# A state-space layer and a gated convolution on one core: weights loaded in smaller pieces, zeros multiplied ahead of the data, and a new order of work

## The chip, the cores and the metric

The kernel runs on 1 core of one Trainium2 chip. The time is the device time of one execution in microseconds. "Span" is the length of the profiled execution in the trace; it is about 1.8 to 1.9 us shorter than the time of the same execution.

## The reference, cut to what matters

Two layers on sequences of 2048 steps and 640 channels, put side by side:

```python
# A: a diagonal complex state space, 640 states
Lam_bar = exp(dt * Lam);  Bu = x @ (B_bar.T)          # complex
for t in range(L): h = Lam_bar * h + Bu[:, t];  hs.append(h)
y_a = 2.0 * real(hs @ C.T) + x * Dskip
# B: a four-tap shift convolution of k, times v, then a 2048-long causal convolution
kv  = sum_t shift(k, t) * shift_k[:, t] * v
y_b = q * (causal_conv(kv, ssm_k) + kv * ssm_D)
return concatenate([y_a, y_b], -1)
```

Three things are enough. Side A needs x transposed, multiplied by B ("B products"), and the results of neighbouring steps joined by small products with rotation matrices M (powers of Lam_bar). Those matrices are built on the chip, in *sets*. Side B needs the shift convolution on VectorE and then many 64-wide products ("s1", "s2", "i1", "i2") on TensorE with two tables R and W.

## The kernel before

The kernel gives every operation a name and a function. A text, ORDER, then lists all of them; each engine works through its own operations in that order. A letter behind a slash chooses the engine (A ACT, D VectorE, G GpSimd, S SyncE for DMAs), and a number behind @ a buffer.

```python
def place(self, text):
    for word in text.split():
        word, _, slots = word.partition("@")
        name, _, e = word.partition("/")
        o = ops[name]
        o.eng = letter[e] if e else next(iter(o.alts))
        assert o.deps <= done, name
        ...
```

The operations that the argument touches:

```python
# ci1: one large integer product on GpSimd, for the cosine tables
self.op("ci1", {"POOL": 2.4}, lambda e: self.nc.gpsimd.tensor_tensor(out=civ(0), in0=civ(0), in1=..., op=ALU.mult), r=["ph"], ...)

# a set: five rotation matrices, two inputs from SBUF, on VectorE or GpSimd
def f(e, h):
    self.eng[e].tensor_tensor(out=mt[:, js, :]..., in0=E[:]..., in1=sap()[:, js, :]..., op=ALU.mult)
for h in range(parts):
    op(f"set_{key}_{h}", alts, lambda e, h=h: f(e, h), r=["E", dep], w=[f"M_{key}_{h}"])

# a unit of side A: ten B products twice (dn0, dn1), an eviction (e1), three rotations (m1), an eviction (e3)
op(f"dn{b}_{u}", {"PE": mm_cost(512, 5)}, f, r=[f"B{h}", f"x{hf}{b}", "Qz", "Bfree"], w=[f"pu{b}_{u}"], bufs=[pt], ...)
self.evac(f"e1_{u}", 768, ...)
op(f"m1_{u}", {"PE": 0.335}, f1, r=[f"h_{u}", f"M_1_{h}", f"M_2_{h}", f"M_3_{h}"], w=[f"pu1_{u}"], ...)
self.evac(f"e3_{u}", 256, ...)

# B through the transposing DMA, in two halves
for h in range(2):
    for u, ap in enumerate((self.A_B_re, self.A_B_im)):
        ...  # nc.sync.dma_start_transpose(out=self.BT[:, :, u, 320 * h:320 * h + 320], in_=ap[320 * h:320 * h + 320, :]...)

# side B's table for group G: its load (hst) and a tap added to it (dtap), which the s1 products wait for
op(f"hst{G}", {"SP": 0.4, "POOL": 1.2}, lambda e: self.eng[e].dma_start(...), w=[f"sth{G}"], ...)
op(f"dtap{G}", {"POOL": 0.26, "DVE": 0.1}, lambda e: self.eng[e].tensor_tensor(..., op=ALU.add), r=["Dm"], w=[f"sth{G}"], ...)
```

"wm0" is a scaling of half of a 64-wide table for W, "den" six tiny operations that lead to the last set, "sk", "cv", "cs" and "ca" the shift convolution.

## Time and profile before

| | before |
|---|---|
| time, median of 3 runs | 202.42 us (200.48 to 203.7) |
| span of the profiled run | 200.5 us |
| TensorE busy | 185.7 us (93%) |
| first B product starts | 11.93 us |
| first rotation (L231) starts | 19.93 us |
| gaps of TensorE behind that | 4.05 us |
| last matmul ends | 196.80 us |

The prediction below shows the page, TensorE's waits and the chain, and reads them. In the timeline (start and duration in us, engine, line, operation, tiles, shapes, count) these rows of VectorE and GpSimd come from the time just ahead of the first rotation and behind it:

```profile
14.70 0.75 DVE L492 TENSOR_TENSOR R<-vs,mk 128x256 bf16<-128x256 f32 x2
16.54 2.63 DVE L422 TENSOR_TENSOR M<-E,ss 128x640 bf16<-128x640 bf16 x2
19.09 0.95 DVE L239 CAST hb<-ps 128x768 bf16<-128x768 f32 x1
...
18.50 4.21 POOL L422 TENSOR_TENSOR M<-E,ss 128x640 bf16<-128x640 bf16 x3
...
33.12 0.17 DVE L387 TENSOR_TENSOR den<-lpar 128x10 f32<-128x10 f32 x1
```

R's two halves take 0.75 us together, done before GpSimd starts with its sets. "den" waits until 33 us, behind the whole convolution of the first group, and takes 0.17 us for its first operation. In the same trace the two operations of wm0 stand from 7.63 us on and take 0.81 and 0.69 us.

### The profile page before, as it was taken

How to read it: one execution, taken by the hardware profiler on the slowest of the kernel's cores; microseconds unless marked ns; L12 is line 12 of the kernel's file. 1: busy time of each engine (PE TensorE's matmuls, PEld its weight loads, DVE VectorE, ACT ScalarE, POOL GpSimd, SP SyncE). 2: the span in 40 equal slices, each digit the busy share in tenths (PEclk: the TensorE clock that was granted, in tenths of full speed). 3: DMA queues.
4: the chain of work that ended last, by engine and by line, in shares of the span. 5: the costliest groups of instructions: out<-in, count | busy, mean ns of one | idle time of the engine just before them, and what ended most of it. 6: DMA issues, size and time to landing. Idle time of an engine off the chain costs nothing.

```text
span 200.5 us, 8859 instructions
## 1 busy us (share of the span) xinstructions
PE 185.7 (93%) x4043; PEld 136.3 (68%) x4043; DVE 168.1 (84%) x264; ACT 148.1 (74%) x175; POOL 20.6 (10%) x35
## 2 busy tenths in 40 slices
PE   0599999979999999699999999999999999999982
PEld 0465566747777678467657777676787878788771
DVE  7899899876899999949988899788959999877540
ACT  4979998978899888389986749896967679752011
POOL 8056500700000000000000000100000010001010
PEclk9999999999999999999999999999999999999999
DMA  5999997999999999969995068509334334998985
GB/s 167 239 152 132 231 180 167 245 159 210 219 180 171 167 217 206 247 153 215 210 196 133 5 152 252 134 22 189 89 147 103 96 80 105 170 234 160 229 226 140
DMA packets 109959, 33.74 MB, mean 168 GB/s; under 512 B 107106, under 2 KB 108642, under 8 KB 109922
## 3 DMA queue, kind: packets, MB, share of 16 engines
q1 hardware_dynamic: 109668, 32.52, 83.9%
q8 instruction: 31, 0.51, 1.1%
q0 software_dynamic: 224, 0.66, 0.9%
q14 instruction: 6, 0.05, 0.1%
q10 hardware_dynamic: 30, 0.00, 0.0%
HBM read 9.19 MB, written 7.86 MB: 85 GB/s over the span
## 4 chain that ended last, share of the span: by engine, by line
PE 72%; DMA 14%; DVE 6%; ACT 3%; SPq 2%; issue 1%; POOL 0%; DVEq 0%; POOLq 0%; ACTq 0%
PE ps L806 20%; PE ps L658 17%; PE ps L909 9%; PE ps L945 8%; PE ps L231 4%; DMA s<-s 4%; PE ps L1001 4%; DMA s<-in_B_v_dram 4%; PE ps L233 4%; PE ps L1037 3%; DMA s<-in_A_x_dram 3%; DMA s<-in_B_ssm_k_dram 3%; DVE s L239 2%; PE ps L810 2%; ACT s L237 2%
## 5 line engine op out<-in xcount | busy, mean ns | idle before, releaser
L237 ACT CAST s<-ps 128x1024 bf16<-128x1024 f32 x86 | 84.1, 1018 | 16.9 <-PE ps L945 6.4
L658 PE MATMUL ps<-xT,BC 128*64 128x512 bf16 x400 | 49.1, 383 | 0.1
L806 PE MATMUL ps<-BC,hb 128*128 128x320 bf16 x240 | 36.4, 300 | 0.0
L658 PEld LDWEIGHTS <-BC 128*64 128x64 bf16 x400 | 22.3, 110 | 15.1 <-issue 0.9
L806 PEld LDWEIGHTS <-hb 128*128 128x128 bf16 x240 | 21.9, 98 | 8.7 <-issue 0.3
L968 DVE TENSOR_TENSOR s<-s,s 128x2048 bf16<-128x2048 bf16 x20 | 24.4, 1222 | 2.0 <-ACT s L237 0.7
L909 PE MATMUL ps<-R,s 64*64 64x128 bf16 x1280 | 22.5, 218 | 2.9 <-POOL s L831 1.8
L237 ACT CAST yo<-ps 128x640 bf16<-128x640 f32 x12 | 8.4, 698 | 22.7 <-PE ps L810 18.5
L909 PEld LDWEIGHTS <-s 64*64 64x64 bf16 x1280 | 18.7, 107 | 8.1 <-issue 3.7
L239 DVE CAST s<-ps 128x1024 bf16<-128x1024 f32 x14 | 17.0, 1220 | 8.3 <-PE ps L909 2.7
L945 PE MATMUL ps<-s,Wre 128*64 128x128 bf16 x320 | 21.4, 221 | 0.0
L763 DVE TENSOR_TENSOR hb<-ps,hb 128x512 bf16<-128x512 f32 x30 | 19.1, 684 | 2.8 <-PE ps L231 1.6
L945 PE MATMUL ps<-s,Wim 128*64 128x128 bf16 x320 | 21.2, 219 | 0.0
L945 PEld LDWEIGHTS <-Wre 128*64 128x64 bf16 x320 | 18.2, 110 | 2.5 <-issue 0.5
L884 DVE TENSOR_TENSOR s<-s,s 128x2048 bf16<-128x2048 bf16 x15 | 18.3, 1222 | 1.0 <-ACT s L876 0.7
L945 PEld LDWEIGHTS <-Wim 128*64 128x64 bf16 x320 | 18.1, 110 | 1.1
L1044 DVE TENSOR_TENSOR s<-ps,s 128x1024 bf16<-128x1024 f32 x10 | 11.8, 1216 | 4.1 <-PE ps L1037 3.9
L237 ACT CAST hb<-ps 128x768 bf16<-128x768 f32 x17 | 13.7, 808 | 1.1 <-PE ps L658 1.1
L968 DVE TENSOR_TENSOR s<-s 128x1024 bf16<-128x1024 bf16 x20 | 13.8, 688 | 0.3
L231 PE MATMUL ps<-hb,M 128*64 128x256 bf16 (+1 forms) x136 | 13.3, 296 | 0.0
L1037 PE MATMUL ps<-Ct,s 128*64 128x64 bf16 x640 | 11.6, 196 | 0.8 <-DMA s<-s 0.7
L1037 PEld LDWEIGHTS <-s 128*64 128x64 bf16 x640 | 11.1, 113 | 1.9 <-DMA s<-s 0.9
(157 smaller groups left out, 261.4 us busy)
## 6 DMA issues: line engine op xcount, KB each, us to landing
s<-in_B_ssm_k_dram SPq DMA_DIRECT2D x5, 512.0 KB, 4.7
kvd<-s SPq DMA_DIRECT2D x5, 512.0 KB, 4.4
s<-kvd SPq DMA_DIRECT2D x5, 512.0 KB, 5.6
s<-in_B_q_dram SPq DMA_DIRECT2D x5, 512.0 KB, 4.4
out_dram<-s SPq DMA_DIRECT2D x5, 512.0 KB, 5.1
out_dram<-yo SPq DMA_DIRECT2D x12, 160.0 KB, 2.8
s<-in_A_x_dram SPq DMA_DIRECT2D x2, 640.0 KB, 4.8
out_dram<-yo POOLq DMA_DIRECT2D x4, 160.0 KB, 3.4
```

The source lines that it names most:

```text
L231: self.nc.tensor.matmul(out[h], lhsT=lhsT[:, h], rhs=rhs, **k)
L237: self.nc.scalar.copy(out=out, in_=in_)
L239: self.eng[e].tensor_copy(out=out, in_=in_)
L658: nc.tensor.matmul(P[64 * ri:64 * ri + 64, b, :], lhsT=self.BT[:, k, ri, 64 * j:64 * j + 64], rhs=self.xT[:, k, hf, 2 * b:2 * b + 2, :].re ...
L763: v.tensor_tensor(out=hv(r), in0=self.P(p2)[:, 0, :].rearrange("p (h m) -> p h m", h=2), in1=hv(r), op=ALU.add)
L806: nc.tensor.matmul(P[:, part, 0:320], lhsT=hap(j), rhs=self.CT[:, j, c0:c0 + 320], start=(j == 0), stop=False)
L884: op(f"ca{j}{G}{h}", {"DVE": dve_tt(W_)}, lambda e, c=c, tt=tt: v.tensor_tensor(out=c(), in0=c(), in1=tt(), op=ALU.add), r=[f"tm{G}{h}"], ...
L909: nc.tensor.matmul(P[64 * ri:64 * ri + 64, r, 128 * b4:128 * b4 + 128], lhsT=d[64 * r:64 * r + 64, 4 * qd + b4, a0, :], rhs=self.R[64 * r: ...
L945: nc.tensor.matmul(P[64 * pi:64 * pi + 64, ri, 128 * k4:128 * k4 + 128], lhsT=W[:, kp, pi, :], rhs=A[:, kp + 16 * pi, :], start=True, stop ...
L968: v.tensor_tensor(out=o, in0=a, in1=b, op=op_)
L1037: nc.tensor.matmul(P[64 * ah:64 * ah + 64, b // 8, 64 * (b % 8):64 * (b % 8) + 64], lhsT=Z[:, 16 * h + b, 64 * ri:64 * ri + 64], rhs=self. ...
L1044: v.tensor_tensor(out=o, in0=self.P(pt)[:].rearrange("p s (b a c) -> p a (s b) c", b=8, a=16), in1=o, op=ALU.mult)
```

## The change

Its intent: start TensorE's clock with products of zeros while x is still on its way; load the first half of B in two pieces so that x's second half comes earlier; and use an order for all engines that was found with VectorE and GpSimd excluding each other at SBUF.

```diff
@@ setup @@
+        warm = self.g.buf("P", "warm", 1)
+        def f_warm(e):
+            for _ in range(8):
+                nc.tensor.matmul(self.P(warm)[:, 0, :], lhsT=self.xT[:, 0, 1, 0, 0:128], rhs=self.xT[:, 0, 1, 0:2, :]..., start=True, stop=True)
+        op("wz", {"POOL": 0.45, "DVE": 0.3}, lambda e: self.eng[e].memset(self.xT[:, 0, 1, 0:2, :], 0.0), w=["x10", "x11", "wz"])
+        op("warm", {"PE": 1.9}, f_warm, r=["wz", "x10", "x11"], w=["warm"], bufs=[warm], due=-35)
@@ a_B @@
-        for h in range(2):
+        for h, (lo, n) in enumerate(((0, 128), (128, 192), (320, 320))):
...
@@ a_unit @@
-  r=[f"B{h}", ...
+  r=[f"B{0 if j < 2 else 1 if j < 5 else 2}", ...
@@ ORDER: all of it is new; the words from the phases to the first taps @@
-x121 fi mk rn ph ci1 ld_sk/S dn0_2_0@4 x130 ex10/D trig dn0_0_0@6 B11 ex14/D ws1@4 R dn1_2_0 rc ss dn1_1_0@0 set_3_0/D
-set_2_0/G dn1_0_0 e1_2_0/A dn1_4_0@2 set_1_0/D ws0@5 k0@6 kz0/G set_1_1/G x131 dn0_4_0 e1_0_0/D hst0/S@2 m1_2_0 x120 set_3_1/G
-dn0_1_0 e3_2_0/D e1_4_0/D m1_0_0 dn1_8_0@4 ct@3 set_2_1/G e3_0_0/D e1_1_0/D dn0_8_0 sk x101 cv300/D@4 dn1_9_0@6 set_4_1/D
-m1_1_0 dn0_9_0 cs200/D@3 v0@5 e1_8_0/A dtap0/D set_8_1/D m1_4_0 e3_1_0/A m1_8_0 e3_4_0/A ca200 s1h03@0,4 ...
+B00 ex10/D ph dn0_2_0@4 ex14/D Dm1/S Ct ld_sk/S trig B20 dn0_4_0@6 ex12/D ws1@3 rc dn1_4_0 ss wm0 dn1_2_0 B21 dn1_1_0@2
+e1_4_0/D e1_2_0/A dn0_1_0 x120 set_2_0/D R dn0_0_0@0 x100 den x110 e1_1_0/D x101 hst0/S@4 ws0@5 kz2/G@6 ci1 set_3_0/G
+set_8_0/G set_1_0/G set_12_0/G m1_4_0 m1_2_0 set_2_1/G dn1_0_0 e3_2_0/D e3_4_0/A m1_1_0 sk e1_0_0/A dn0_9_0@4 cs200/D@2 ct@3
+cv300/D@3 dn1_3_0@6 x130 ca200 dn1_9_0 e3_1_0/D cs100/D dn0_3_0 set_3_1/D dn1_8_0@2 e1_9_0/A ca100 x131 e1_3_0/A m1_0_0
+e3_0_0/D x121 x111 v0@1 kz1/G@5 set_4_1/G set_1_1/G set_8_1/G set_12_1/G set_4_0/G m1_9_0 dn0_8_0 e3_9_0/D dtap0/G cs000/D
...
```

## The prediction

> **What bounds the kernel now.** I read the page first (its busy shares), then TensorE's waits, then the chain that ended last, then the timeline of the head, where the change is aimed.
>
> ```profile
> PE 185.7 (93%) x4043; PEld 136.3 (68%) x4043; DVE 168.1 (84%) x264; ACT 148.1 (74%) x175; POOL 20.6 (10%) x35
> PE ps L607 <- DMA s<-in_A_x_dram: 7.0, 2, 5.0
> PE ps L909 <- POOL s L831: 1.8, 1, 1.8
> PE ps L909 <- ACT s L237: 1.1, 1, 1.1
> PE ps L1037 <- DMA s<-s: 0.7, 1, 0.7
> ```
>
> The kernel is TensorE-bound: 185.7 of 200.5 us busy. The waits account for nearly all the rest: 5.0 us until the first half of x lands, 2.0 for its second half, 1.8 at 82 us, 1.1 at 43 us, 0.7 near the end, and 3.7 us from the last matmul (196.8 us) to the span's end. So a new order can win only (a) the head, (b) the gaps at 43, 82 and 191 us, (c) time in which TensorE is busy but slow.
>
> The head, from the chain of waits and the timeline:
>
> ```profile
> 4.19 5.45 DMA s<-in_A_x_dram
> 9.68 2.31 PE ps L607 x20
> 11.99 8.10 PE ps L658 x35
> 20.09 0.33 PE ps L231 x3
> ```
>
> ```profile
> 1.54 1.23 POOL L577 IOTA s<- 128x1280 int32 x1
> 1.63 1.33 DVE L461 TENSOR_SCALAR phs<-ws,rowa 128x32 int32<-128x32 int32 x2
> ...
> 11.50 2.33 POOL L578 TENSOR_TENSOR s<-s,ph 128x1280 int32<-128x1280 int32 x1
> 11.55 2.31 DVE L487 TENSOR_SCALAR mk<-mk 128x4 f32<-128x4 f32 x1
> ...
> 16.59 1.90 POOL L422 TENSOR_TENSOR M<-E,ss 128x640 bf16<-128x640 bf16 x1 [2.76 <-DVE ss L412]
> ```
>
> Two things to see. TensorE never stops between 9.68 us and 42.5 us, but it starts slow: 20 transposes take 2.31 us. Counted by window, L658:
>
> ```profile
> 11.92:13.00 1.08, 1.07 (x6) 0.49 (x8) 1.00 1.17 156
> 13.02:14.10 1.08, 1.08 (x12) 0.55 (x10) 1.00 1.28 257
> ```
>
> (matmuls in parentheses): 6 in the first 1.08 us, 12 in the next, while the granted-clock column says 1.00 in both. So there is a cold start which that column does not show. And VectorE is held[...]: a tensor_scalar of four elements a partition takes 2.31 us beside a 2.33 us GpSimd product and ends with it, where its neighbours take 0.15 us.
>
> **What the Trainium skill says.** "TensorE: Matmul & The Clock Gate", Part 1: the array runs at half clock until a free-running window of about 3.4 us has been busy, and the matmuls issued until then run cold. The trace agrees: transposes start every 0.107 us up to 11.7 us, and from 13 us on, pairs of 512-column matmuls start every 0.216 us instead of the first ones' 0.427. Part 4 of that page says transposes do not count as activity; this trace rather speaks against it, since only 0.9 us of ordinary matmuls precede the speed-up at about 12.8 us. "SBUF — State Buffer", "SBUF: two separate sides": GpSimd and VectorE share a port pair under an exclusive lock, held for a whole instruction, against VectorE's two-port modes and, for GpSimd operations that read SBUF, two-input ones. The rows above agree; so does a set product on GpSimd, 1.90 us beside VectorE's own and 1.25 us alone (at 20.2 us). The same section warns that descriptors of DMAs issued from GpSimd are held by that lock; the few such transfers of before (3.4 us to landing against 2.8 from SyncE for the same output tiles) show it at most weakly.
>
> **The change, part by part.**
>
> *Zeros ahead of the data.* One memset (about 0.2 us, VectorE, at about 1.1 us) and eight 512-column matmuls. Cold, they start every 0.427 us: 8 x 0.427 = 3.4 us, from about 1.3 to 4.8 us, inside the 5.0 us wait, so free. They do not delay x. With the transposes that follow from 5.0 us the array should be at full speed at some point between 5 and 8 us, depending on where the window lies. What was cold in before: 40 transposes x (0.107 - 0.054) = 2.1 us and two pairs x 0.21 = 0.4 us. The first 20 are followed by a wait for x anyway, so on the path are 20 x 0.053 + 0.4 = 1.5 us.
>
> *B's first half in two pieces.* In before 320 rows (0.41 MB) of B go between x's two halves on the DMA queue; now 192 rows (0.25 MB). Transposes moved about 0.28 MB/us, so 0.6 us less stands in front, and SyncE's issue of that piece falls from 1.97 us to about 1.2 (192/320). x's second half should land at about 8.2 us instead of 9.68, with a wide margin. The remaining 128 rows are first needed after four products of 1.08 us. So the first B product can start at about 8.2 + 1.1 (20 warm transposes) + 0.2 = 9.5 us instead of 11.9: 2.4 us earlier.
>
> *The order.* I read it engine by engine. TensorE's operations are the same but for the zeros. I count changes between tilings (64-column, 64-row, full) along its sequence: 82 in before, 72 now. In the chain each change costs about 0.11 us (ten matmuls of L658 take 1.20 us after L909 against 1.08 after their own kind; L806 1.47 against 1.36): 10 x 0.11 = 1.1 us saved. The transfer of the third h tile (512 KB), which left SyncE at 78.1 us and caused the 1.8 us gap at 82, now stands ahead of two C pieces and of the first Z transpose in SyncE's list: that gap should close. Between ACT and VectorE 26 evacuations and scalings go one way and 14 the other; eleven set and tap operations go from VectorE to GpSimd, two back. My sum is about +2 us on VectorE and -6 on ACT: neither becomes the bound. Ten DMA issues move from SyncE to GpSimd, four back.
>
> *What limits the head gain.* In both orders seven B products (7 x 1.08 = 7.6 us) come before the first rotation (L231), which needs the rotation matrices M. In before it started at 19.93 us without a wait, the last M having come at 19.17. Now M for shift 1 is third on GpSimd's list after the scales ss are known: 3 x 1.25 = 3.8 us, up to 1.9 each where VectorE holds the lock. Working forward along VectorE's new list (set-up operations pushed behind GpSimd's iotas, the wm scaling ahead of the phases), I get the phases at about 11.3 us. GpSimd's big product then holds the lock to about 13.8, the two-input Ct products wait for it, and behind them stand x's third evacuation, the products rc and then ss, at 14.5 to 16.5 us. Hence the first rotation at 18.5 to 22.5 us, middle 20.3, against 19.93: TensorE gets its B products done earlier and then waits for M. The 2.4 us won ahead of it are probably lost again there.
>
> **Sum.** From the first rotation to the last matmul before took 196.8 - 19.9 = 176.9 us, of which 4.0 were gaps: 172.9 of work, now 171.8. New end = 20.3 + 171.8 + gaps + 3.7 = 195.8 + gaps. If the gaps at 82 and 43 us go and one or two new ones of a microsecond come (GpSimd's long row of sets before the first tap, the second h tile through GpSimd's queue), the gaps are about 3 us: span 198.8. The timed figure is about 1.9 us above the span (202.4 against 200.5), which gives 200.7. Against that stands that such an order was searched for with the exclusion in view, so the search has probably placed the head better than my hand does: with the rotation at 18.0 and gaps of 2 us the span is 195.5 and the time 197.4. I take a point between them, 198.8.
>
> **The rivals.**
>
> *A: the head is won whole.* VectorE gets through between GpSimd's operations, M comes by 17.5 us, TensorE runs on from 9.5 us. For it: small VectorE operations (one element per partition) ran beside iotas unhindered in before. Against it: 2.31 us for four elements. It would make 20.3 into 17.2 and the time 194 to 197.
>
> *B: the lock becomes the wait.* Eleven sets and taps on GpSimd (12.5 to 19 us) lie beside the shift convolution on VectorE (about 10 us of lock) from 16 to 35 us; the first tap (dtap) ends late, and the first s1 products, now at about 31 us on TensorE, wait for it, or the convolution is late and the k side waits. For it: 1.90 against 1.25 us. Against it: the first s1 products were put some 4 us later in the order. It would make 200 to 203.
>
> *C: a transfer issued by GpSimd is late.* The second h tile, needed at about 43 us, and group 4's store and reload near 150 us now go through GpSimd. For it: the third h tile's lateness cost 1.8 us in before. Against it: group 4's have some 8 us of slack. One miss costs 1 to 3 us.
>
> *D: the tail decides.* Before's last Z transpose takes 8.8 us from issue to use and is covered by about 9.3 us of projections and i1 products; the new order puts the same work there, so I expect the tail unchanged.
>
> **Range and chances.** Rival A's lower half gives 194.8, B with a late transfer 202.2. The 2% line is 198.4, close under my point: faster 0.43, same 0.51, slower 0.06 (a search that ended above the old order would have been dropped, but I cannot see what it was measured on).
>
> **What would show it.** L607's transposes should start every 0.054 us for x's second half, and the first L658 near 9.5 us. A wait of TensorE for M (L422) or for x's evacuation between 11 and 21 us means the head was lost as I say; none, and the first L231 under 18.5 us, means A. The wait on L831 at 82 us should be gone. VectorE operations stretched beside L422 on GpSimd between 16 and 35 us, with a TensorE wait behind them, mean B; waits on L831 or L909 for a GpSimd-issued DMA mean C. I am wrong in the sum if TensorE's gaps after the first rotation are under 1 or over 5 us.

## More of the kernel before

In the table of stretches (busy time, and number of instructions, of PE, PEld, DVE, ACT and POOL; then granted clock, DMA share, GB/s), TensorE has no pause here:

```profile
20.00:25.00 5.00, 5.00 (x56) 2.88 (x54) 4.36 (x9) 4.97 (x5) 2.71 (x3) 1.00 1.11 232
25.00:30.00 5.00, 5.00 (x156) 3.46 (x156) 4.58 (x7) 4.77 (x8) 0.11 (x1) 1.00 1.18 184
```

## The result, and the profile after

| | before | after |
|---|---|---|
| time, median of 4 runs of the same rounds | 202.64 us (200.48 to 203.7) | 210.32 us (209.29 to 211.05) |
| span, profiled run | 200.5 | 208.8 |
| first B product | 11.93 | 10.80 |
| first rotation | 19.93 | 19.88 |
| TensorE's gaps behind that | 4.05 | 10.44 |
| TensorE's work behind that | 172.82 | 174.50 |
| last matmul to the end | 3.68 | 3.98 |

The change is slower: ratio 1.041, 95% interval 1.031 to 1.051. A ratio is the mean time of one kernel's runs over that of the other's of the same rounds, so not quite the ratio of the medians quoted here. Executions over 1.5% slower than the fastest of the same kernel are left out of the means.

The last four rows add up to the span, and so give the account of the 8.3 us: first rotation -0.05, gaps +6.39, work +1.68, tail +0.30. "Work" is what is left of the time from the first rotation to the last matmul when the gaps are taken out. Two thirds of the loss is one gap. TensorE's waits in after (line, released by, us in total, times, longest):

```profile
PE ps L232 <- DVE hb L240: 5.5, 1, 5.5
PE ps L615 <- DMA s<-in_A_x_dram: 2.1, 1, 2.1
PE ps L916 <- ACT s L238: 1.6, 3, 1.1
...
PE ps L1044 <- DMA s<-s: 1.3, 1, 1.3
```

A rotation (L232) waited 5.5 us for an eviction on VectorE (L240): e1_1_0, one cast of 768 columns. The chain of waits from 15 us to that rotation tells why. Its columns are start, us, and what ran:

```profile
15.20 1.86 DVE s L536
17.09 1.63 DVE s L537
18.71 0.86 DVE hb L240
19.58 0.93 DVE M L431
20.50 2.79 DVE R L501 x2
23.30 1.14 DVE den L396
...
24.55 1.12 DVE den L398
...
26.95 0.88 DVE hb L240
27.87 0.85 PE ps L232 x6
```

It is VectorE alone, one operation behind the other: wm0 (L536, L537), an eviction, a set, R, den, and only then the eviction that TensorE stands still for. The set-up operations among them are far longer than in before, the two evictions (0.94 us each in the timeline, against 0.95) are not: wm0 1.86 and 1.63 us (0.81 and 0.69), R 2.79 for two (0.75), the first den 1.14 (0.17). What runs on GpSimd meanwhile:

```profile
15.25 7.77 POOL L431 TENSOR_TENSOR M<-E,ss 128x640 bf16<-128x640 bf16 x5 [2.10 <-DVE ss L421]
...
23.02 6.26 POOL L431 TENSOR_TENSOR M<-E,ss 128x640 bf16<-128x640 bf16 x5
```

Ten sets without a pause, from 15.25 to 29.28 us. Taking each VectorE operation of 15.2 to 29.3 us less its duration where GpSimd is still, VectorE loses 8.1 us in these 15 (wm0 1.98, R 2.12, the den group 2.76, the cast of sk 1.08, the set 0.18). This is the exclusion; the order that was found with it in view puts VectorE's set-up into the middle of it, and an eviction behind that.

The wait has a second price. In the table of stretches (columns as above) the granted clock falls after it, and once more near the beginning:

```profile
10.00:15.00 5.00, 5.00 (x38) 2.53 (x37) 4.28 (x13) 4.95 (x9) 2.70 (x3) 0.66 0.84 148
...
20.00:25.00 5.00, 1.99 (x22) 1.14 (x21) 4.97 (x6) 4.93 (x6) 5.00 (x5) 1.00 0.70 143
25.00:30.00 5.00, 2.13 (x14) 1.52 (x15) 4.89 (x8) 2.03 (x2) 4.51 (x5) 0.74 0.94 201
```

TensorE is busy for 1.99 and 2.13 us of 5 where before had 5.00 and 5.00. The records of the clock give half speed from 10.30 to 13.71 us and from 27.36 to 30.78. In the second stretch TensorE works from 27.87 on, 2.9 us at half speed: 1.45 us lost, nearly the whole +1.68 of "work". The first half-speed stretch follows the wait of 2.06 us for x's second half; it eats what the zeros had won, since the B products up to 13.4 us start every 0.427 us a pair again. That first stretch is not in every execution, and it does not set the end: a_fix below, with the same list for TensorE, waited 1.52 us there, kept the full clock, and reached its first rotation at 19.80 us against 19.88.

### The profile page after: what moved, and what is told of

Read it like the earlier page. It is cut to its first block, busy times and chain, and to the rows that moved or that the text cites.

```text
span 208.8 us, 8879 instructions
## 1 busy us (share of the span) xinstructions
PE 190.8 (91%) x4044; PEld 137.2 (66%) x4044; DVE 174.3 (83%) x268; ACT 142.2 (68%) x163; POOL 35.1 (17%) x50
## 4 chain that ended last, share of the span: by engine, by line
PE 76%; DVE 9%; DMA 7%; ACT 3%; issue 2%; SPq 1%; DVEq 0%; ACTq 0%
PE ps L813 19%; PE ps L665 17%; PE ps L952 9%; PE ps L916 9%; PE ps L232 5%; PE ps L1008 5%; DMA s<-s 5%; PE ps L234 5%; PE ps L1044 4%; DMA s<-in_A_x_dram 3%; PE ps L817 2%; ACT s L238 1%; DVE R L501 1%; PE ps L793 1%; DVE s L240 1%
## 5 line engine op out<-in xcount | busy, mean ns | idle before, releaser
L238 ACT CAST s<-ps 128x1024 bf16<-128x1024 f32 x88 | 85.6, 1020 | 22.5 <-PE ps L916 9.6
L665 PE MATMUL ps<-xT,BC 128*64 128x512 bf16 x400 | 50.5, 395 | 0.0
L665 PEld LDWEIGHTS <-BC 128*64 128x64 bf16 x400 | 23.8, 115 | 16.4 <-issue 2.9
L952 PE MATMUL ps<-s,Wre 128*64 128x128 bf16 x320 | 20.9, 220 | 0.1
L238 ACT CAST yo<-ps 128x640 bf16<-128x640 f32 x9 | 6.3, 696 | 21.3 <-PE ps L817 19.2
L238 ACT CAST hb<-ps 128x768 bf16<-128x768 f32 x15 | 12.1, 805 | 12.5 <-PE ps L665 12.4
L240 DVE CAST s<-ps 128x1024 bf16<-128x1024 f32 x12 | 14.7, 1222 | 2.7 <-PE ps L952 1.1
L232 PE MATMUL ps<-hb,M 128*64 128x256 bf16 (+1 forms) x124 | 11.2, 290 | 5.9 <-DVE hb L240 5.5
L431 POOL TENSOR_TENSOR M<-E,ss 128x640 bf16<-128x640 bf16 x10 | 14.0, 1433 | 2.1 <-DVE ss L421 2.1
L232 PEld LDWEIGHTS <-M 128*64 128x64 bf16 x160 | 7.9, 111 | 8.5 <-issue 5.8
```

The source lines that it names most:

```text
L232: self.nc.tensor.matmul(out[h], lhsT=lhsT[:, h], rhs=rhs, **k)
L238: self.nc.scalar.copy(out=out, in_=in_)
L240: self.eng[e].tensor_copy(out=out, in_=in_)
L431: self.eng[e].tensor_tensor(out=mt[:, js, :].rearrange("p j (r i) -> p j r i", r=2), in0=E[:].rearrange("p (a b i) -> p a b i", a=1, b=1). ...
L665: nc.tensor.matmul(P[64 * ri:64 * ri + 64, b, :], lhsT=self.BT[:, k, ri, 64 * j:64 * j + 64], rhs=self.xT[:, k, hf, 2 * b:2 * b + 2, :].re ...
L952: nc.tensor.matmul(P[64 * pi:64 * pi + 64, ri, 128 * k4:128 * k4 + 128], lhsT=W[:, kp, pi, :], rhs=A[:, kp + 16 * pi, :], start=True, stop ...
```

## The experiments

The expectations name theories, some by number. Theory 1 is the one just told: GpSimd's row of sets holds VectorE, and evictions stand behind what is held. Theory 2 is that VectorE's own order and load are to blame, with GpSimd adding little. Theory 3 is that the wait can be removed and is taken back later, since something else sets the end. Theory 4 is that the second table's load, issued by GpSimd behind its sets, is another bound, hidden by the first wait. Theory 6 is that the new order as such costs, with the sets where before had them. The remaining ones were narrower rivals: that the load alone is the bound (rival 5), that this one eviction is on the wrong engine, that the place of R and den ahead of it is all of it, that the new parts (zeros, three pieces of B) cost. Each expectation gives its own figures.

All kernels are correct. "After" and "before" name the kernel that was edited; an order is edited by moving words. Line numbers shift by up to nine between the kernels (the eviction at L240 in after is at L239 in the experiments).

### One eviction on the other engine: a_evac_act

```diff
-den x110 e1_1_0/D x101
+den x110 e1_1_0/A x101
```

> The changed kernel with one eviction, e1_1_0 (L240, 128x768, the one that TensorE waited 5.50 us for at 27.87), given to ScalarE, which idled there. Theory 1 (GpSimd's ten set products hold the port, VectorE's two R products and three den products wait behind them, and the eviction waits behind those in VectorE's queue): the wait falls under 1.5 us, TensorE's half clock of 27.36 to 30.78 us goes too, the span falls from 208.8 by 5 to 7 us to about 202.5. Theory 2 (VectorE's own order and load make it late, the port adds little): the same, so this run doesn't part 1 from 2. Theory 3 (the head's wait is taken back later, something else sets the end): the wait goes but the span falls by less than 2 us.

Measured 209.77 us, ratio 1.045 (1.039 to 1.050), span 208.5: nothing won. TensorE now waits for the next thing in VectorE's queue, and the clock still halves, from 27.85 to 31.27 us:

```profile
PE ps L664 <- DVE Qb L239: 3.2, 2, 2.4
```

The eviction behind it (e3_2_0) starts at 26.88 us, at the same time as e1_1_0 did. So the misplaced thing is not one eviction but the whole held queue ahead of it; the expected gain missed: the span fell by 0.3 us.

### Fewer sets beside it: a_sets_late

```diff
-set_8_0/G set_1_0/G set_12_0/G ... set_4_1/G set_1_1/G set_8_1/G set_12_1/G set_4_0/G ... set_G_1/G ... hst1/G@0
+set_1_0/G ... set_1_1/G ... set_G_1/G set_8_0/G set_12_0/G set_4_1/G set_8_1/G set_12_1/G set_4_0/G ... hst1/G@0
```

VectorE's order is untouched. The six moved sets are first read at 79.6 us of this trace.

> The changed kernel with six of GpSimd's set products (4, 8 and 12, both halves), which nothing needs before 70 us, moved behind the two sets of G; VectorE's order is untouched. Theory 1 (port): the two R products take 0.4 us each instead of 1.47, the den products 0.16 instead of 1.1, the eviction e1_1_0 starts at 22 to 23.5 us instead of 26.88, TensorE's wait falls from 5.50 to under 2 us, its clock doesn't drop, and the span falls by 4 to 7 us. Theory 2 (VectorE's order alone): the wait stays over 4 us. Theory 3: the wait shrinks, the span falls by less than 2 us.

Measured 215.06 us, ratio 1.071 (1.063 to 1.078). The head did what theory 1 says, with the same VectorE list:

```profile
20.55 0.75 DVE L500 TENSOR_TENSOR R<-vs,mk 128x256 bf16<-128x256 f32 x2
21.22 0.16 DVE L395 TENSOR_TENSOR den<-lpar 128x10 f32<-128x10 f32 x1
...
PE ps L915 <- DVE s L837: 9.1, 1, 9.1
PE ps L231 <- DVE hb L239: 1.9, 2, 1.6
```

R takes 0.75 us again, den's first operation 0.16, e1_1_0 starts at 23.05 instead of 26.88, and the 5.5 us wait is 1.56. This is the direct test of cause, and theory 2 falls with it: only GpSimd's list differs. The time is worse through my edit: the sets stand ahead of the second table's load (hst1), which GpSimd therefore issued at 45.92 us instead of 41.99, and TensorE waited 9.1 us, until 53.7 us, for the tap on that table (L837), with half clock from 48.4 to 58.6 us.

### R and den behind the evictions: a_vorder

```diff
-set_2_0/D R dn0_0_0@0 x100 den x110 e1_1_0/D ... e3_0_0/D ... cs000/D
+set_2_0/D dn0_0_0@0 x100 x110 e1_1_0/D ... e3_0_0/D R ... cs000/D den
```

> The changed kernel with R put behind the eviction e3_0_0 and den behind the product cs000 in VectorE's order, GpSimd untouched: the port is as busy as before, but the eviction e1_1_0 no longer stands behind the operations it holds. Theory 1 and 2: e1_1_0 starts at about 20.5 us, TensorE's wait for it goes, the half clock with it, span about 202.5; the R and den products may still be stretched where they now stand, and if s1's first product (needed at about 31 us) waits for R, up to 2 us come back. Theory 3: less than 2 us.

Measured 209.11 us, ratio 1.042 (1.036 to 1.049). The 5.5 us wait and the half clock behind it are gone, and hardly anything is won (span 206.9, 1.9 us less, which is theory 3's figure): what stands there instead, the convolution, is held in turn.

```profile
22.92 3.36 DVE L884 TENSOR_SCALAR s<-s,sk 128x2048 bf16<-128x2048 bf16 x2
26.32 2.16 DVE L890 TENSOR_TENSOR s<-s,s 128x2048 bf16<-128x2048 bf16 x1
...
PE ps L664 <- DVE Qb L239: 1.9, 1, 1.9
```

The pair at L884 takes 1.42 us and the sum at L890 1.23 where GpSimd is still. Waits of 1.87 us at 28.9, 1.31 at 32.0 and 1.68 at 48.6 take the place of the one. With the ten sets left where they are, what VectorE had next paid for them here.

### The parts without the order: b_both, b_zeros

Before's own order; b_zeros has the zeros alone, b_both the three pieces of B as well (with the change's code for them):

```diff
-scol pidx Dm0 B00 ... zero J1 ... B01 ... B10 ... B11
+scol wz/D pidx Dm0 B10 ... zero warm@0 J1 ... B11 B00 B01 ... B20 ... B21
```

> The kernel before, in its own order, with the two other parts of the change alone: B's first half in two pieces (192 rows where the 320 were, the 128 rows right behind) and the zeros ahead. Theory 1 says that the loss is of the order alone: x's second half still comes at about 9.4 us, its transposes run mostly at full speed, TensorE gets 0.5 to 1 us earlier into the products and then waits for the set matrices at about 19.2 to 19.9 us as before, so the span is 199.5 to 201.5, within 1 per cent of 200.5. Rival: the parts themselves cost (more transfers in front of x, the clock dropping again in the wait for x): over 202.5.

> The kernel before with the zeros alone. x's second half lands at 9.7 us as before; its 20 transposes take about 1.2 us instead of 2.3 unless the clock drops again in the 2 us wait (then about the same as before); then TensorE gets up to 1.5 us ahead and loses it at x's third evacuation, which VectorE makes at 13.8 to 14.8 behind a product held by GpSimd, and at the sets of 19.2 to 19.9. Span 199.5 to 201, like b_both. If the zeros paid for themselves in full: 199 or less.

Measured: b_both 201.94 us, ratio 1.005 (0.999 to 1.011), span 199.3; b_zeros 201.44 us, ratio 0.997 (0.989 to 1.006), span 197.9. The new parts are not the loss. They are hardly a gain either, though TensorE's first B product starts at 9.55 us (b_both) and 9.73 (b_zeros) instead of 11.93: in both the first rotation stays at 19.9 us, because TensorE then waits for an x eviction that stands behind VectorE's held "mk" (2.31 us beside ci1): 2.61 us at 14.5 us in b_both, 1.6 us in b_zeros. The span of b_zeros is that of its fastest run (199.69 us; the other three took 200.38 to 202.56).

No run shows that the split of B brings x's second half earlier. Its transposes start at 9.68 us in before, but at 8.42, 8.51 and 8.68 in three more traces without the split (b_gpsets, b_zeros, bz_ci1late), and between 8.33 and 9.69 in those with it. The scatter from run to run is about as large as the 1.5 us that the split was to win.

### The second table's load through SyncE: a_hst1_sp

```diff
-hst1/G@0
+hst1/S@0
```

> The changed kernel with the load of the second h tile (hst1) issued by SyncE instead of GpSimd, where it stood behind the ten sets and the two of G (issued at 41.99 us, used by VectorE at 48.32). Theory 4 (two bounds one behind the other: first VectorE held by the sets, then this load; each hides the other): alone it changes little, the span stays within 1.5 us of 208.8 and the 5.50 us wait stays, since VectorE reaches its tap late anyway. Rival 5 (the load by GpSimd is the real bound of the first 60 us): the span falls by over 3 us.

Measured 209.49 us, ratio 1.037 (1.032 to 1.042), span 207.9. The 5.50 us wait stays as it was and hides this one, as theory 4 expected; rival 5 falls.

### Both: a_sets_late2 and a_fix

a_sets_late2 moves the six sets behind hst1 on GpSimd; a_fix has hst1 by SyncE besides (`hst1/S@0`).

```diff
-set_8_0/G ... set_12_0/G ... set_4_1/G ... set_8_1/G set_12_1/G set_4_0/G ... hst1/G@0
+hst1/G@0 set_8_0/G set_12_0/G set_4_1/G set_8_1/G set_12_1/G set_4_0/G
```

> As a_sets_late, but the six late sets now stand behind hst1 on GpSimd, so that they don't hold up its issue (in a_sets_late it left at 45.92 and TensorE waited 9.15 us for the tap behind it). Theory 4: the head is as in a_sets_late (R products 0.41, den 0.16 to 1.1, longest wait before 50 us about 1.6), hst1 leaves at about 37 us, the wait for the tap is under 2 us, no half clock after 20 us; span 200.5 to 204. Theory 3 (something else sets the end): over 206.

> Both: the six sets behind, and hst1 by SyncE. Theory 4: both bounds gone, span 199 to 202.5, at most 1 us off the kernel before; better than a_sets_late2 by 0 to 2 us. If it stays over 204, the order has a third bound that I haven't seen.

Measured: 206.97 us, ratio 1.025 (1.021 to 1.029), span 205.5; and 205.55 us, ratio 1.019 (1.015 to 1.022), span 203.5. Both missed their range on the slow side, but a_fix recovers 5.3 of the 8.3 us of span with the same VectorE list as after. What is left:

```profile
PE ps L231 <- DVE hb L239: 2.2, 3, 1.6
PE ps L915 <- DVE s L837: 1.6, 1, 1.6
...
44.83 1.28 DVE L837 TENSOR_TENSOR s<-s,Dm 128x16 bf16<-128x16 bf16 x1
```

The second tap (L837), 0.23 us elsewhere, takes 1.28 us beside the six sets in their new place (36.8 to 46.0 us), and the convolution ahead of it is held too. The sets were moved, and so was part of the loss.

### The distribution of the sets in the old order: b_gpsets

Before's order, with ten sets in a row on GpSimd behind ss as in after (kz0 behind set_1_0, both G sets on GpSimd):

```diff
-ss dn1_1_0@0 set_3_0/D set_2_0/G ... set_1_0/D ... set_1_1/G ... set_3_1/G ... set_2_1/G ... set_4_1/D ... set_8_1/D ...
+ss set_3_0/G set_8_0/G set_1_0/G kz0/G@6 set_12_0/G set_2_1/G set_4_1/G set_1_1/G set_8_1/G set_12_1/G set_4_0/G dn1_1_0@0 set_2_0/D ... set_3_1/D ...
```

> The kernel before, in its own order, with the set products distributed as the changed kernel has them: ten in a row on GpSimd from the scales on, two on VectorE, both of G on GpSimd; nothing else. VectorE is relieved of 6.6 us of work (8 x 0.82). Theory 1 (held port): the shift convolution's products beside them are stretched by 0.5 to 1.3 us each from 16 to 33 us, M for shift 1 comes at 20 to 21.5 us instead of 19.2, TensorE waits there and behind a late tap or eviction; span 202 to 206. Rival (GpSimd is free help and the loss is in the rest of the order): 200.5 or less.

Measured 205.78 us, ratio 1.018 (1.013 to 1.023), span 203.5. As expected: putting the sets on GpSimd costs about 3 us in the old order too.

```profile
PE ps L231 <- POOL s L841: 1.5, 1, 1.5
...
25.32 3.30 DVE L878 TENSOR_SCALAR s<-s,sk 128x2048 bf16<-128x2048 bf16 x2
```

The first rotation waits for its set (the releaser named is a memset of 0.1 us that runs right behind set_1_0) and starts at 21.56 us; the convolution's L878 pair, 1.42 us uncontended, takes 3.30. The tap, at 28.54 us, takes 1.28.

### The six sets back on VectorE: a_fix2

After with hst1 by SyncE, three of the six sets behind the convolution's end (cm10) on VectorE, three behind the scan.

```diff
-set_8_0/G set_1_0/G set_12_0/G ... set_4_1/G set_1_1/G set_8_1/G set_12_1/G set_4_0/G ... hst1/G@0 ... cm10 ... scan0
+set_1_0/G ... set_1_1/G ... hst1/S@0 ... cm10 set_4_0/D set_8_0/D set_12_0/D ... scan0 set_4_1/D set_8_1/D set_12_1/D
```

> The changed kernel with hst1 by SyncE and the six late sets on VectorE, three behind the second convolution and three behind the scan. In a_fix they stood on GpSimd from 36 to 45 us and held VectorE's two scalings and the tap there (1.44, 1.74 and 1.28 us instead of 0.75, 0.75 and 0.23), and TensorE waited 1.59 us for the tap at 46.17. Theory 1: that wait goes, the 1.56 us at 24 stays (wm, set 2 and den are still held by the first GpSimd sets); span 200.5 to 202.8, against 203.5. If the wait at 46 stays, it wasn't the port.

Measured 208.08 us, ratio 1.028 (1.024 to 1.033), span 206.4: missed. The tap's wait went as expected, but three sets in a row on VectorE made new waits, 1.48 us at 54.8 and 1.55 at 85.3, and the head of this run had half clock until 14.8 us.

### The large product later in the old order: b_best, bz_ci1late

The large GpSimd product ci1 moves from ahead of "mk" to behind set_1_1; b_best has zeros and three pieces of B besides, bz_ci1late the zeros alone.

```diff
-ph ci1 ld_sk/S ... set_2_0/G ... set_1_1/G x131
+ph ld_sk/S ... set_2_0/G ... set_1_1/G ci1 x131
```

> The kernel before with zeros and the split, and GpSimd's big product (ci1, 2.3 us) moved behind the first three GpSimd sets, so that it no longer holds VectorE's last mk operation, behind which x's second and third evacuation, R and the scales stood. Theory 1: mk takes 0.2 us instead of 2.3, the scales ss come about 2 us earlier, the first rotation at 17.5 to 18.5 us instead of 19.9, TensorE's wait of 2.6 us before the third B product goes; span 197.3 to 199 against 199.3 (b_both). If GpSimd's product then holds something else as long, 199 to 201.

> As b_best without the split of B: zeros and the moved product. If the split does nothing (b_both 201.9 against b_zeros 201.4 in time, within noise), the same as b_best within 0.7 us; if the split brings the second half of x earlier, b_best is ahead by up to 1 us.

Measured: b_best 203.75 us, ratio 1.006 (1.002 to 1.010), span 201.8; bz_ci1late 202.88 us, ratio 1.002 (0.995 to 1.010), span 199.2. In b_best the head does what was expected: "mk" falls from 2.31 us to 0.17, the scales ss are there 2 us earlier, and the first rotation starts at 17.77 us instead of 19.93. The time does not follow, and the expected span was missed:

```profile
11.56 0.17 DVE L495 TENSOR_SCALAR mk<-mk 128x4 f32<-128x4 f32 x1
...
PE ps L915 <- DMA s<-kvd: 1.5, 1, 1.5
...
PE ps L915 <- POOL s L837: 1.2, 1, 1.2
```

TensorE arrives 2 us earlier at loads that have not come as much earlier: 0.8 us for B's imaginary part, 1.5 us for the reload of kv and 1.2 us at a tap. (Before has waits of 1.1 and 1.8 us at the last two places as well.) The gaps after the first rotation are 6.43 us against before's 4.05. The DMA share lies near or above 1 in before's head (1.16, 1.00, 1.03, 1.11, 1.18 in the stretches of five us from 5 to 30), so an early start that the loads do not support is the likely reading; no run tests it. bz_ci1late, the same without the split, ends 0.9 us lower, with overlapping intervals (its profiled run is its fastest).

### The new order with the old distribution: a_oldsets, a_oldsets_wm0

a_oldsets puts the sets on the engines, and about at the places, that before gave them, with hst1 by SyncE; a_oldsets_wm0 also moves wm0 early, behind wm1, as in before.

```diff
-ph ... ss wm0 ... set_2_0/D R ... ci1 set_3_0/G set_8_0/G set_1_0/G set_12_0/G ... set_3_1/D ... set_4_1/G ...
+ph ci1 ... ss set_2_0/G set_1_1/G set_3_1/G set_2_1/G kz2/G@6 set_3_0/D set_1_0/D wm0 ... R ... cv300/D@3 set_4_1/D ... ca100 set_8_1/D ...
```

> The changed kernel with the set products on the engines and at about the places where the kernel before has them (sets 3 and 1 on VectorE right behind the scales, 2, 1, 3, 2 of the halves on GpSimd, the rest one by one on VectorE beside the convolutions), and hst1 by SyncE. Theory 1 (the row of sets on GpSimd is the loss): the wait of 5.50 us becomes under 1.5, span 200.5 to 203.5. Theory 6 (the rest of the new order costs by itself, as a_fix and a_fix2 hint): span 204 to 207 although no wait behind held operations is over 1.5 us.

> As a_oldsets, with the second wm scaling back behind the first, ahead of the phases, so that it isn't held by the sets (1.85 + 1.63 us instead of 0.81 + 0.69) ahead of the first evictions. Theory 1: 1 to 2 us under a_oldsets, 199.5 to 202. Theory 6: within 1 us of a_oldsets.

Measured: 207.43 us, ratio 1.028 (1.021 to 1.034), span 205.1; and 207.15 us, ratio 1.028 (1.021 to 1.035), span 205.1. The spans are theory 6's figures: the distribution alone does not repair the new order. Its condition, no long wait behind held operations, is not met, so this does not show that the order as such costs. In a_oldsets the gaps after the first rotation are down to 4.17 us, before's number, but the rotation itself comes at 22.04 us: its eviction stands behind two sets and wm0, 1.74 and 1.63 us beside the GpSimd sets that are left, a wait of 2.56 us, and the clock halves from 23.0 to 26.4 us. With wm0 early the phases come later instead, x's third eviction starts at 14.83 us behind a held Ct, a wait of 2.59 us comes at 15.6, and the rotation at 22.21.

### After without the zeros: a_nozeros

```diff
-op("wz", ...)
-op("warm", ...)
```

> The changed kernel without the zeros (no memset, no eight products). The first rotation waits for the set matrices at about 19.9 to 20.6 us either way, so the zeros can neither win nor lose behind it: span 208 to 210, within 1 us of 208.8. If the zeros cost (the clock window that they shift lies badly), it falls by over 1.5 us; if they pay even here, it rises by as much.

Measured 211.32 us, ratio 1.048 (1.040 to 1.055), span 209.5, 0.7 us above after's. The zeros neither cause nor cure it.

### All of it together: a_fix3, a_fix4

What the best variant of the new order still lost was open, so two more runs joined the edits. a_fix3 is a_fix with R and den in a_vorder's places; a_fix4 has the six sets one by one on VectorE near their first use instead of in a row on GpSimd.

```diff
-hst1/S@0 set_8_0/G set_12_0/G set_4_1/G set_8_1/G set_12_1/G set_4_0/G ... diagD ... cs220/D ... cs120/D ... scan0 ... jcv0 ... jsv0
+hst1/S@0 ... diagD set_4_0/D ... cs220/D set_8_0/D ... cs120/D set_12_0/D ... scan0 set_4_1/D ... jcv0 set_8_1/D ... jsv0 set_12_1/D
```

> The changed order with the six late sets behind hst1 on GpSimd, hst1 issued by SyncE (both as in the best variant of the new order, span 203.5), and in addition R behind e3_0_0 and den behind cs000 on VectorE. If what is left of the head's waits in that variant (0.6 and 1.6 us at 20 and 24 us) comes from the place of R and den ahead of the eviction e1_1_0, then the wait at 24 us goes, nothing is held in their new place since GpSimd has few sets there, and the span is 201 to 202.2, the time 203.2 to 204.5, ratio about 1.01. If the time is merely paid at the next held operation, as when R and den were moved alone, the span stays at 203 to 204.

> As the run before it, but the six late sets one by one on VectorE near their first use (55 to 95 us) instead of in a row on GpSimd at 37 to 46 us. If the tap's wait at 46 us (1.6 us) comes from those six sets holding cs210 and the tap, it goes and the span falls by another 1 to 1.6 us, to 199.8 to 201, about the kernel before's 200.5; if new waits come at 55 to 95 us as when three stood in a row on VectorE, the span stays above 202.

Measured: a_fix3 205.80 us, ratio 1.020 (1.016 to 1.024), span 202.9; a_fix4 206.17 us, ratio 1.020 (1.015 to 1.025), span 204.4. Neither gains on a_fix in time (the profiled a_fix3 is its fastest run). Inside, each edit did what it should: in a_fix3 the wait at 24 us is gone and nothing of R or den is held, in a_fix4 the six sets no longer hold the tap. But other waits came: in a_fix3 1.81 us at 44.5 for the tap and 1.16 at 49.3, in a_fix4

```profile
PE ps L915 <- DMA s<-kvd: 2.2, 1, 2.2
```

at 50.7 us, for the reload of kv again, with half clock from 51.5 to 54.9, and 1.11 us at 70.9 for a set.

### What the runs tell together

| kernel | first rotation | gaps after it | work | tail | span |
|---|---|---|---|---|---|
| before | 19.93 | 4.05 | 172.82 | 3.68 | 200.48 |
| b_gpsets | 21.56 | 4.60 | 173.66 | 3.68 | 203.50 |
| after | 19.88 | 10.44 | 174.50 | 3.98 | 208.80 |
| a_vorder | 19.85 | 9.46 | 173.64 | 3.98 | 206.92 |
| a_fix | 19.80 | 6.76 | 173.04 | 3.90 | 203.50 |
| a_fix3 | 19.61 | 6.33 | 173.00 | 3.92 | 202.86 |
| a_oldsets | 22.04 | 4.17 | 174.44 | 4.41 | 205.05 |

Each row is one execution, and other runs of a kernel lie up to 3 us from it; the rows of a_vorder, a_fix, a_fix3 and a_oldsets are those of the fastest run of each. Before's own gaps are not fixed either: b_both and b_zeros, in its order, had 2.33 and 1.45 us in place of 4.05.

Some 5 of the 8.3 us (5.3 by the spans, 4.6 by the ratios) are shown to be the early row of sets and the load behind it: they come back when those are moved, with VectorE's list unchanged (a_fix). At least 2.4 us of span are left in every variant of the new order that was tried (2.4 in a_fix3, 3.0 in a_fix, more in the others), at different places each time: VectorE's set-up ahead of evictions, the tap, the reload of kv. How they divide stays open: each edit removed the wait that it was made for and another took its place. No version tried here is shown to beat the kernel before; b_zeros, at 0.997, is not clear of the scatter.

## Why the prediction was wrong

It said 198.8 us, with 194.8 to 202.2 around it, and the time is 210.32.

**The step that failed** is in the sum: "one or two new ones of a microsecond come [...], the gaps are about 3 us". They are 10.44 us, and the prediction named over 5 us as the mark of a wrong sum. One new wait alone is 5.5 us long. The error comes from where the working stopped. The prediction went forward along VectorE's new list up to ss and the first M, to find the first rotation; the next entries, R, den and e1_1_0, stand in the same lists beside the GpSimd row it had counted ("Eleven sets and taps on GpSimd"). Its own row of 2.31 us for an operation of four elements a partition was reason enough to count them as held. Of the other gaps, that at 43 us is still there (1.11 us, now at 56.5; in both traces kv's reload lands within 0.02 us of the end of the eviction that the view names, at 44.19 and 56.46, so either could be what held TensorE). The one at 82 us went as said, but it is absent from b_both and b_zeros too, which keep before's order there, so its going is not shown to be the new order's work.

**Rival B** ("the lock becomes the wait") is the mechanism, at 200 to 203 us. It was looked for at the taps and the convolution from 16 to 35 us, and its 203 us is 4 us above the point. The stretched operations and the TensorE wait behind them are as it says; the waiting thing is an eviction, and the time came out 7 us above the upper end. It also counted on "small VectorE operations ran beside iotas unhindered": that holds for its operations of one element beside iotas, while beside sets two of den's operations on ten elements took 1.1 us in place of 0.17.

**The work** of 171.8 us was 174.5. The half clock after the long wait, 1.45 us, was not foreseen. The 1.1 us for fewer changes of tiling did not appear: the variants without half clock after the first rotation (a_fix 173.04, a_fix3 173.00) have before's work of 172.82 or a little more. Counted again with the operations that take the tiling of their neighbours, the changes in the traces from the first rotation on are 86 against 92, not 72 against 82.

**The head.** The eight zeros run every 0.427 us inside the wait for x and are free, as said; full clock from 6.88 us instead of 12.82, as said. The transposes of x's second half started at 9.37 us, not 8.2; as told above, that time scatters by over a microsecond with the split and without, so the runs neither confirm nor refute the 1.5 us that the prediction gave the split. In this execution the wait for it was 2.06 us, the clock fell again, and the first B product came at 10.80, not 9.5. The first rotation was put at 20.3 and is 19.88 (20.56 for the second of its three products): ci1 to 13.15 us, the held Ct, x's third eviction at 13.42 to 14.10 and ss at 15.17 come in the order that the working has, at most 0.7 us earlier than it says. "The 2.4 us won ahead of it are probably lost again" is right, and b_both shows the same in the old order.

**Rival A** fell. **Rival C** is true in part: the second table's load by GpSimd is a bound, but it shows only when the first wait is gone (a_fix is 1.4 us faster than a_sets_late2). **Rival D**, an unchanged tail, holds within 0.3 us. And the argument that a search with the exclusion in view "has probably placed the head better than my hand does" moved the point from 200.7 to 198.8, in the wrong direction: the working by itself was nearer.

## What to carry to other kernels

When work goes to GpSimd, walk VectorE's list through the *whole* time that GpSimd is at SBUF, and look for what TensorE needs at the end of that list: the evictions themselves were not held here (0.94 us beside sets, 0.95 in before), but they stood behind operations that were. Keep set-up work that is not yet needed out of that stretch on either engine. Price a TensorE wait of over 2 us at more than its length, since the clock may halve for the next 3.4 us; and check an earlier start against when the loads arrive, which scatters from run to run.

## What the Trainium skill lacked or had wrong

- "TensorE: Matmul & The Clock Gate", "Why this matters for your kernels", names, in its table, idle gaps of over about 3 us as what costs the clock. Here shorter ones did. The clock's changes in the traces lie on windows of 3.41 us. Over the 19 traces, all 11 windows at full clock (ahead of the kernel's end) with 2.06 us or more of TensorE idle time were followed by a window at half clock; of 68 with 0.9 to 1.9 us idle, 64 were not. What counts is idle time within one window, not the gap: in b_both a gap of 2.61 us that fell on two windows (1.19 and 1.42 us) cost no clock.
- The same page, Part 4, says that transposes do not count as activity in the same way. The traces agree in part, against what the prediction made of it: the four exceptions above (1.40 to 1.78 us idle, yet half clock next) all lie in the first ten microseconds, in windows that held mostly transposes (another such, 1.77 us idle in a_oldsets_wm0, kept the clock). But in before the window from 9.41 to 12.82 us, with 2.3 us of transposes and 0.9 of ordinary matmuls, was followed by full clock, so they do not count for nothing. Products of zeros count: full clock at 6.88 us in after.
- "SBUF — State Buffer", "SBUF: two separate sides", has the lock right: a set on GpSimd takes 1.25 us alone and up to 1.90 beside VectorE, half of R 0.41 us alone and 1.47 beside sets. It does not draw the consequence: an operation that waits for the port holds back those behind it in VectorE's list, here an eviction out of PSUM, which TensorE then waited 5.5 us for.
- No page that I found shows the lock on a tiny operation, though nothing in the rule exempts one: two-input operations of 128x10 elements took 1.1 us in place of 0.17, and mk (128x4, one input) 2.31 in place of 0.17.
